# A retention layer and a feed-forward in one kernel: the order of work in the two-chunk group and two places in the load queue

## The chip, the cores and the metric

The kernel runs on one core of one Trainium2 chip. The metric is the device time of one execution in microseconds. A core has five engines with an instruction queue each: TensorE (PE; its weight loads are shown as PEld), VectorE (DVE), ScalarE (ACT), GpSimd (POOL) and SyncE (SP). Transfers are issued by POOL or SP and carried out by 16 DMA engines. Each queue runs in its program order, so an instruction that waits holds up all that stand behind it.

## What is computed

```python
B, H, S, D = 4, 8, 768, 64
gamma = 1.0 - 2.0 ** (-5.0 - np.arange(H))
for t in range(S):                                   # linear attention with decay
    state = gamma * state + np.einsum('bhd,bhe->bhde', k[:, :, t], v[:, :, t])
    y[:, :, t] = 1/sqrt(D) * np.einsum('bhd,bhde->bhe', q[:, :, t], state)
x = y.transpose(0, 2, 1, 3).reshape(B * S, H * D)    # 3072 x 512
h = x @ w_in                                         # 512 x 2048
g = h + sin(alpha * h) ** 2 / (alpha + 1e-9)
out = g @ w_out                                      # 2048 x 512
```

All inputs are float32 in memory and are cast to bfloat16 as they are loaded.

## The kernel before

The recurrence is cut into 24 chunks of 128 time steps, six for each of the four batches. `order`, also called `P`, is the order in which chunks are worked on: first the first chunk of every batch (`e0` to `e3`), then the other five of batch 0, of batch 1 and so on. P[n] is the n-th chunk in this order, counted from 0. The feed-forward takes the chunks in groups of 4, 2, 4, 4, 4, 4 and 2; the second group, the two-chunk group, is P[4] and P[5]. While the feed-forward of one group runs, the attention of the next group's chunks is worked in between; during the two-chunk group these are P[6] to P[9].

A chunk passes through these steps:

- `load_chunk` issues three DMAs on POOL's queue, for q, k and v. The last nine wide chunks (`load_seq`) come with eight DMAs for each of q, k and v of a batch. POOL keeps at most eight loads in flight: each issue waits until the eighth last has landed.
- `scale_v` multiplies v by a decay table in place, mostly on POOL, in the same queue as the loads. It waits until v has landed.
- q and k are turned (transposed), either by `turn`, a DMA transpose on SP's queue that waits until k has landed (written `X` in the schedule), or by `stage_T`, eight transposes on PE into the PSUM bank "ty" and a copy by DVE (L251; written `T`).
- `stage_A` (`A`) makes the scores, eight matmuls (L265) into the PSUM tile `pa` of two banks, which DVE multiplies by a mask (L269). For wide chunks `scores` does it (L337).
- `stage_M` (`M`) is the mix: eight matmuls with the state (L299) and eight with the scores (L303) into a tile `py` in the bank "ty", then the update of the state (L279). DVE multiplies `py` by a decay table into `xT`, the input of the feed-forward (L310), and ACT copies the state (L286). `SK` is the update of the state alone, for a chunk whose mix is done earlier.

The feed-forward of a group goes in slots. A slot (class `Slot`) is one or two slices of 128 of the 2048 inner columns: matmuls with `w_in` into a bank `ph` of the tag "mm" (L425), the sine on ACT (L428) and, by `sq`, the square on ACT (L433); `add` is the addition of h on DVE into `gT` (L440, once for each slice). The two-chunk group has eight slots of two slices. `phase` runs a group: for each slot the matmuls, sine and square, then the attention steps listed for this slot, then the slot's additions, then some matmuls with `w_out` (L450) for the group before. The order of the program is the order of every engine's queue; it is written out by hand, and tiles alone decide who waits.

PSUM has eight banks: four of the tag "mm", one "ty", one "ps" and the two of "pa". The "mm" banks hold the slots' `ph` and the output sums `po`; a new tile takes the bank that came free first. In the program's order the next group's first `ph` takes the bank of slot 5, the first output sum of the two-chunk group that of slot 6, and the next group's second `ph` that of slot 7.

The scores of a chunk of the next groups, P[10], P[11], P[12] and P[13], are made in slots 1, 5, 8 and 11 of the third group, those of P[14] in its slot 14, and those of P[15], the first wide chunk, in slot 2 of the fourth.

Of the kernel before, what the change touches and what calls it, by code (L numbers as in the profile page):

```python
# [8 lines left out]
F32 = mybir.dt.float32  # L9
# [6 lines left out]
def kernel(  # L16
# [15 lines left out]
    nc = tc.nc  # L32
# [4 lines left out]
    NP = H // 2  # L37
# [20 lines left out]
    psum = ctx.enter_context(tc.tile_pool(name="psum", bufs=1, space=bass.MemoryType.PSUM))  # L58
# [10 lines left out]
    def chunk_of(t, j):  # L69
        b, c = divmod(j, NCH)  # L70
        return t[b, :, c * C:(c + 1) * C, :].rearrange("h s d -> s h d")

    def load_chunk(j, names="qkv"):
        for name, src in (("q", q), ("k", k), ("v", v)):
            if name not in names:
                continue
            if name == "v":
                t = big.tile([128, H, D], BF16, name="vr", tag="vr", bufs=NJ - 9)
            else:
                if ("qk", j) not in raw:  # L80
                    raw["qk", j] = big.tile([128, 2, H, D], BF16, name="qkr", tag="qkr", bufs=NJ - 10)
                t = raw["qk", j][:, "qk".index(name)]
            nc.gpsimd.dma_start(out=t, in_=chunk_of(src, j))  # L83
            raw[name, j] = t

    def wide(j):
        return j >= 2 * NCH + 2 and j != 3 * NCH
# [45 lines left out]
    def scale_v(j, eng):  # L133
        t, by = raw["v", j], kg
        if wide(j):
            t, by = t.rearrange("i f p d -> i (f p) d"), kgq
        eng.tensor_mul(t, t, by[:, j % NCH, :, None].to_broadcast([128, H, D]))  # L137
# [103 lines left out]
    def stage_T(j, eng=None, tag="ty"):  # L241
        pt = psum.tile([128, 2 * NP, 128], BF16, name="pt", tag=tag, bufs=4 if tag == "mm" else 1)
        st["qkT", j] = work.tile([128, 2 * NP, 128], BF16, name="qkT", tag="qkT", bufs=6)
        for i in range(2):
            for p in range(NP):
                nc.tensor.transpose(pt[:, i * NP + p, :],
                                    raw["qk"[i], j][:, 2 * p:2 * p + 2, :].rearrange("p h d -> p (h d)"), ident)
        if eng is nc.scalar:
            nc.scalar.copy(st["qkT", j], pt)
        else:  # L250
            nc.vector.tensor_copy(st["qkT", j], pt)  # L251

    def turn(j):

        st["qkT", j] = work.tile([128, 2 * NP, 128], BF16, name="qkT", tag="qkT", bufs=6)
        nc.sync.dma_start_transpose(out=st["qkT", j], in_=raw["qk", j].rearrange(
            "i a f p d -> i (a f p d)" if wide(j) else "i a h d -> i (a h d)"))

    def stage_A(j):
        qkT = st["qkT", j]  # L260
        pa = psum.tile([128, 2, NP, 128], F32, name="pa", tag="pa")
        for p in range(NP):
            for e in range(2):
                r = slice(64 * e, 64 * e + 64)
                nc.tensor.matmul(pa[:, e, p, :], qkT[r, NP + p, :], qkT[r, p, :],  # L265
                                 start=(p == 0), stop=True, skip_group_check=True)
        aT = work.tile([128, 2, NP, 128], BF16, name="aT", tag="aT", bufs=2)
        m = dec.rearrange("p e n t -> p (e n) t") if j % NCH == 0 else mask_bc
        nc.vector.tensor_mul(aT.rearrange("p e n t -> p (e n) t"), pa.rearrange("p e n t -> p (e n) t"), m)  # L269
        st["aT", j] = aT  # L270

    def stage_S(j):
        c = j % NCH
        if c == 0:
            st["ps"] = psum.tile([128, NP, D], F32, name="ps", tag="ps")
        ps = st["ps"]
        for p in range(NP):
            for e in range(2):
                nc.tensor.matmul(ps[64 * e:64 * e + 64, p, :], raw["k", j][:, 2 * p + e, :], raw["v", j][:, 2 * p + e, :],  # L279
                                 start=(c == 0 and p == 0), stop=True, skip_group_check=True)  # L280
        return ps

    def keep_S(j, ps):
        for e in range(2):
            r = slice(64 * e, 64 * e + 64)
            nc.scalar.copy(s_bd[(j % NCH + 1) % 2][r, :, r], ps[r, :, :])  # L286

    def stage_M(j):
        c = j % NCH
        g, i = place[j]  # L290
        if g not in xT:
            xT[g] = work.tile([128, KS, sizes[g] * C], BF16, name="xT", tag="xT", bufs=3)
        qkT, aT, vs = st["qkT", j], st["aT", j], raw["v", j]
        py = psum.tile([128, NP, 128], F32, name="py", tag="ty")
        if c > 0:
            for p in range(NP):
                for e in range(2):
                    r = slice(64 * e, 64 * e + 64)
                    nc.tensor.matmul(py[r, p, :], s_bd[c % 2][:, p, r], qkT[:, p, :],  # L299
                                     start=(p == 0), stop=True, skip_group_check=True)  # L300
        for p in range(NP):
            for e in range(2):
                nc.tensor.matmul(py[64 * e:64 * e + 64, p, :], vs[:, 2 * p + e, :], aT[:, e, p, :],  # L303
                                 start=(c == 0 and p == 0), stop=True, skip_group_check=True)
        x = xT[g][:, :, i * C:(i + 1) * C]
        if c == 0:
            nc.scalar.copy(x, py)  # L307
            return
        ps = stage_S(j) if c < NCH - 1 else None
        nc.vector.tensor_mul(x, py, qg[:, c])  # L310
        if ps is not None:
            keep_S(j, ps)
# [90 lines left out]
    def run(more, *kinds):  # L403
        for kind in kinds:
            if more and kind in more:
                more.pop(kind)()
# [76 lines left out]
    def out_pieces(g, tss):  # L483
        return [lambda ts=ts, f=f: ff_out(g, ts, f) for ts in tss for f in range(FF)]
# [13 lines left out]
    e0, e1, e2, e3 = order[:B]  # L498
# [17 lines left out]
    half_T(e1, 1, nc.vector)  # L516
    nc.tensor.transpose(pal, alpha_row, ident_f)
    stage_M(e0)
    grow(1)
    idle_work(1)  # L520
# [4 lines left out]
    idle_work(2)  # L525
    half_T(e2, 1, nc.vector)
    stage_M(e1)
    grow(3)
    nc.scalar.copy(alpha_sb, pal)
# [4 lines left out]
    decay_table(1)  # L534
    idle_work(5)
    stage_M(e2)
    decay_table(2)
    idle_work(3)
# [1 line left out]

    rest = [{}]

    def phase(g, outs, att, nf=1):


        no, done = len(outs), 0
        for n in range(FF // nf):
            more, fresh = rest[0], {}
            now = Slot(g, n * nf, nf=nf).sq("A")
            run(more, "keep", "exit", "hand")  # L550
            for fn in att.get(n, ()):
                fresh.update(fn() or {})
            run(fresh, "mask")
            if fresh:
                rest[0] = fresh
            now.add()
            while done < no * (n + 1) * nf // FF:
                outs[done]()
                done += 1

    def T(j):
        return lambda: stage_T(j)

    def X(j):
        return lambda: turn(j)

    def A(j):
        return lambda: stage_A(j)

    def M(j):  # L570
        return lambda: stage_M(j)

    def SK(j):
        return lambda: keep_S(j, stage_S(j))
# [3 lines left out]
    P = order  # L578
# [9 lines left out]
    outs = out_pieces(0, (2, 3))  # L588
# [83 lines left out]
    scale_v(P[6], nc.gpsimd)  # L672
    load_chunk(P[9])
    scale_v(P[7], nc.gpsimd)
    load_chunk(P[10])
    scale_v(P[8], nc.gpsimd)
    scale_v(e1, nc.gpsimd)
    for n in range(11, 15):
        scale_v(P[n - 2], nc.gpsimd)
        load_chunk(P[n])  # L680
    load_seq(2, "q")
# [21 lines left out]
    stage_M(P[5])  # L703
    fill(4)
    phase(1, outs,
          {0: [X(P[8])], 1: [A(P[6])], 2: [T(P[7]), X(P[9])], 3: [A(P[7]), M(P[6])], 4: [X(P[10])],
           5: [A(P[8]), M(P[7])], 6: [X(P[11]), A(P[9]), M(P[8]), SK(e1)], 7: [M(P[9])]}, 2)

    where = {10: (2, 1)}
    for g in range(2, NG - 1):  # L710
# [35 lines left out]
    for g in range(2, NG):  # L746
        phase(g, out_pieces(g - 1, range(sizes[g - 1])), atts[g], 1 if sizes[g] > 2 else 2)
# [31 lines left out]
```

## Time and profile before

| | |
|---|---|
| time, median of 3 runs | 215.21 us (214.86 to 215.47) |
| span of the profiled execution, first to last instruction | 214.1 us |
| median time less this span (the profiled execution's own time is not listed apart) | 1.1 us |
| PE busy in the span | 204.8 us, 96% |
| two-chunk group, slots | 48.3 to 65.0 us |
| third group | 65.0 to about 96 us |
| granted clock of PE | 1.00 in all these stretches |
| share of the 16 DMA engines, 48.28 to 65.00 and 65.00 to 95.36 us | 1.89 and 1.95 (packets overlap on an engine, so that it exceeds 1) |

In the rows of the timeline the first two figures are the start and the length in microseconds, then come engine, line of the program, operation, what it writes and reads, and the shapes. What stands in brackets is the engine's idle time ahead of it and who ended that. A trailing x8 means that eight instructions in a row are merged. A row of the table by stretches has the stretch, its length, then the busy time of PE, PEld, DVE, ACT and POOL with the number of instructions, the granted clock, the share of the DMA engines and GB/s.

### The profile page before, as it was taken

The numbers are of one execution on the slowest core, as the hardware profiler recorded it, in microseconds if no ns is written. First come the engines' busy times: TensorE is split into PE (matmuls) and PEld (weight loads), VectorE is DVE, ScalarE is ACT, GpSimd is POOL, SyncE is SP. The second block draws the span as 40 slices with busy tenths as digits, with TensorE's granted clock in tenths as the row PEclk, the third lists the DMA queues.
The fourth block names the chain that finished last, engine by engine and source line by source line (L and its number), as shares of the span: only waits on it lengthen the run. The fifth ranks groups of instructions, "written<-read, shape, count | busy, mean of one in ns | idle before, by whom it ended". The sixth has DMA issues, their size and how long they took to land.

```text
span 214.1 us, 4691 instructions
## 1 busy us (share of the span) xinstructions
PE 204.8 (96%) x1849; PEld 109.2 (51%) x1849; DVE 131.8 (62%) x249; ACT 160.2 (75%) x303; POOL 103.5 (48%) x136
## 2 busy tenths in 40 slices
PE   7698899999999999999999999999999999999994
PEld 3344554457664555544554554554545444655653
DVE  4877859964896777746745756665744644433310
ACT  7588696758889988897697796677678787666631
POOL 8965434899679869999997103203300100000000
PEclk9999999999999999999999999999999999999999
DMA  9999999999999999999999842131011101111112
GB/s 127 147 193 186 206 207 171 154 135 229 163 148 201 126 142 187 94 147 198 170 162 145 123 98 70 32 98 54 0 51 52 40 9 52 49 49 52 49 49 98
DMA packets 101189, 24.95 MB, mean 117 GB/s; under 512 B 93728, under 2 KB 98224, under 8 KB 101168
## 3 DMA queue, kind: packets, MB, share of 16 engines
q0 software_dynamic: 77360, 13.38, 83.6%
q1 hardware_dynamic: 23664, 11.22, 25.7%
q8 instruction: 14, 0.23, 0.4%
q10 hardware_dynamic: 144, 0.07, 0.1%
q14 instruction: 7, 0.06, 0.1%
HBM read 27.27 MB, written 6.29 MB: 157 GB/s over the span
## 4 chain that ended last, share of the span: by engine, by line
PE 79%; DVE 9%; ACT 7%; DMA 3%; issue 2%; DVEq 0%; ACTq 0%
PE po L450 34%; PE ph L425 31%; ACT s L428 4%; DVE aT L269 3%; PE spare L492 3%; DMA qkT<-qk_seq 3%; DVE gT L440 2%; ACT s L433 2%; PE pa L265 2%; PE poh L473 2%; PE py L299 1%; PE py L303 1%; PE pa L337 1%; PE py L327 1%; DVE xT L310 1%
## 5 line engine op out<-in xcount | busy, mean ns | idle before, releaser
L440 DVE SCALAR_TENSOR_TENSOR gT<-s,rec_alpha,ph 128x512 bf16<-128x512 f32 (+3 forms) x120 | 74.2, 638 | 64.9 <-ACT s L433 64.8
L425 PE MATMUL ph<-xT,w_in 128*128 128x512 bf16 (+3 forms) x480 | 98.0, 336 | 0.4 <-DVE gT L440 0.2
L450 PE MATMUL po<-w_out,gT 128*128 128x512 bf16 x368 | 95.3, 380 | 0.4 <-ACT xT L307 0.3
L428 ACT ACTIVATE s<-ph,alpha_sb 128x512 f32<-128x512 f32 (+3 forms) x120 | 69.6, 601 | 34.0 <-PE ph L425 33.7
L425 PEld LDWEIGHTS <-w_in 128*128 128x128 bf16 x480 | 45.6, 98 | 41.9 <-issue 1.4
L433 ACT ACTIVATE s<-s 128x512 f32<-128x512 f32 (+1 forms) x94 | 58.4, 621 | 2.6
L450 PEld LDWEIGHTS <-gT 128*128 128x128 bf16 x368 | 33.9, 98 | 36.4 <-issue 0.6
L391 POOL CAST s_bd<-s_f 64x256 bf16<-64x256 f32 x10 | 3.9, 394 | 39.5 <-DVE s_f L384 30.1
L462 ACT COPY o_sb<-po 128x512 f32<-128x512 f32 x23 | 13.2, 579 | 4.0 <-PE po L450 3.9
L83 POOL DMA_DIRECT2D vr<-in_v_dram x15 | 13.7, 914 | 3.4 <-DMA w_in<-in_moe_w_in_dram 1.7
L83 POOL DMA_DIRECT2D qkr<-in_q_dram x14 | 12.8, 917 | 3.8 <-DMA w_out<-in_moe_w_out_dram 1.6
L137 POOL TENSOR_TENSOR vr<-vr,kg 128x512 bf16<-128x512 bf16 x12 | 12.7, 1071 | 3.8 <-DMA vr<-in_v_dram 3.3
L83 POOL DMA_DIRECT2D qkr<-in_k_dram x14 | 12.5, 896 | 3.7 <-DMA w_out<-in_moe_w_out_dram 3.3
L269 DVE TENSOR_TENSOR aT<-pa,mask 128x1024 bf16<-128x1024 f32 x11 | 13.4, 1218 | 0.5 <-PE pa L265 0.5
L103 POOL DMA_DIRECT2D qk_seq<-in_q_dram x16 | 11.3, 741 | 2.9 <-DMA qkr<-in_k_dram 1.2
L137 POOL TENSOR_TENSOR v_seq<-v_seq,kgq 128x512 bf16<-128x512 bf16 x9 | 9.4, 1071 | 4.0 <-DMA v_seq<-in_v_dram 3.7
L103 POOL DMA_DIRECT2D v_seq<-in_v_dram x16 | 11.3, 776 | 0.0
L103 POOL DMA_DIRECT2D qk_seq<-in_k_dram x16 | 11.2, 743 | 0.0
L492 PE MATMUL spare<-warm 128*128 128x512 bf16 x28 | 9.5, 462 | 1.2 <-DVE warm L156 1.2
L286 ACT CAST s_bd<-ps 64x256 bf16<-64x256 f32 x24 | 8.7, 361 | 2.3 <-PE ps L279 2.1
L346 DVE TENSOR_TENSOR aTw<-pa,maskq 128x768 bf16<-128x768 f32 x9 | 8.6, 955 | 0.7
L310 DVE TENSOR_TENSOR xT<-py,qg 128x512 bf16<-128x512 f32 x11 | 7.5, 685 | 1.8 <-PE py L303 1.7
(92 smaller groups left out, 143.0 us busy)
## 6 DMA issues: line engine op xcount, KB each, us to landing
out_dram<-o_sb SPq DMA_DIRECT2D x23, 256.0 KB, 2.2
w_in<-in_moe_w_in_dram POOLq DMA_DIRECT2D x4, 512.0 KB, 11.3
w_out<-in_moe_w_out_dram POOLq DMA_DIRECT2D x4, 512.0 KB, 14.9
vr<-in_v_dram POOLq DMA_DIRECT2D x15, 128.0 KB, 7.0
qkr<-in_q_dram POOLq DMA_DIRECT2D x14, 128.0 KB, 7.0
qkr<-in_k_dram POOLq DMA_DIRECT2D x14, 128.0 KB, 7.4
qk_seq<-in_q_dram POOLq DMA_DIRECT2D x8, 80.0 KB, 6.7
qk_seq<-in_k_dram POOLq DMA_DIRECT2D x8, 80.0 KB, 4.6
```

The lines of the kernel that those rows point to most:

```text
L83: nc.gpsimd.dma_start(out=t, in_=chunk_of(src, j))
L103: nc.gpsimd.dma_start(out=o, in_=src[bt, h, cs[0] * C:, :].rearrange("(f i) d -> i f d", i=64))
L137: eng.tensor_mul(t, t, by[:, j % NCH, :, None].to_broadcast([128, H, D]))
L269: nc.vector.tensor_mul(aT.rearrange("p e n t -> p (e n) t"), pa.rearrange("p e n t -> p (e n) t"), m)
L310: nc.vector.tensor_mul(x, py, qg[:, c])
L425: nc.tensor.matmul(self.ph[:, m, :], w_in[:, i, f * 128:(f + 1) * 128], xT[g][:, i, self.lo:self.hi], start=(m == 0 and i == 0), stop=(i = ...
L428: nc.scalar.activation(out=self.s[:, m, :], in_=self.ph[:, m, :], func=ACTF.Sin, scale=alpha_sb[:, f:f + 1])
L433: nc.scalar.activation(out=self.s, in_=self.s, func=ACTF.Square)
L440: nc.vector.scalar_tensor_tensor(gT[self.g][:, f, self.lo:self.hi], self.s[:, m, :], rec_alpha[:, f:f + 1], self.ph[:, m, :], op0=ALU.mult ...
L450: nc.tensor.matmul(po[g, ts], gT[g][:, f, ts * C:(ts + 1) * C], w_out[:, f, :], start=(f == 0), stop=(f == FF - 1))
L462: nc.scalar.copy(o_sb, po[g, ts])
L492: nc.tensor.matmul(spare["ps"], warm[:, :128], warm, start=True, stop=True)
```

## The change

It does four things, all in or ahead of the two-chunk group.

- The mix of P[9], the last one in the group (slot 7), takes its PSUM tile from the tag "pa", the scores' two banks, and no longer from "ty".
- The additions of slot 6 are held back: `phase` keeps them and issues them in slot 7 after that slot's attention steps, so behind the multiplication that ends the mix of P[9], and ahead of slot 7's own additions.
- P[7] (the chunk `T` stands for; the eighth chunk counted from one) is turned by PE in slot 0 instead of slot 2.
- In POOL's queue the three loads of P[10] are put behind the scalings of v of P[8], of `e1` and of P[9]. Those of P[11] still follow them, now behind P[10]'s; the scaling of P[10] comes after both.

```diff
-    def stage_M(j):
+    def stage_M(j, tag="ty"):
...
-        py = psum.tile([128, NP, 128], F32, name="py", tag="ty")
+        py = psum.tile([128, NP, 128], F32, name="py", tag=tag)
...
-    def phase(g, outs, att, nf=1):
+    def phase(g, outs, att, nf=1, late=None):
...
+        held = None
...
-            now.add()
+            if held is not None:
+                held.add()
+                held = None
+            if n == late:
+                held = now
+            else:
+                now.add()
...
     scale_v(P[7], nc.gpsimd)
-    load_chunk(P[10])
     scale_v(P[8], nc.gpsimd)
     scale_v(e1, nc.gpsimd)
-    for n in range(11, 15):
+    scale_v(P[9], nc.gpsimd)
+    load_chunk(P[10])
+    load_chunk(P[11])
+    for n in range(12, 15):
         scale_v(P[n - 2], nc.gpsimd)
         load_chunk(P[n])
...
     phase(1, outs,
-          {0: [X(P[8])], 1: [A(P[6])], 2: [T(P[7]), X(P[9])], 3: [A(P[7]), M(P[6])], 4: [X(P[10])],
-           5: [A(P[8]), M(P[7])], 6: [X(P[11]), A(P[9]), M(P[8]), SK(e1)], 7: [M(P[9])]}, 2)
+          {0: [X(P[8]), T(P[7])], 1: [A(P[6])], 2: [X(P[9])], 3: [A(P[7]), M(P[6])], 4: [X(P[10])],
+           5: [A(P[8]), M(P[7])], 6: [X(P[11]), A(P[9]), M(P[8]), SK(e1)],
+           7: [lambda: stage_M(P[9], "pa")]}, 2, 6)
```

## The prediction, made before the changed kernel ran

> **What bounds the kernel now.** I read the engines' busy shares first, then the busy table by stretches, then the timeline of the two-chunk group (48.3 to 65.0 us) and of the stretch behind it.
>
> ```profile
> PE 204.8 (96%) x1849; PEld 109.2 (51%) x1849; DVE 131.8 (62%) x249; ACT 160.2 (75%) x303; POOL 103.5 (48%) x136
> 48.28:65.00 16.72, 15.99 (x217) 11.53 (x216) 13.27 (x24) 14.26 (x33) 13.43 (x15) 1.00 1.89 180
> 65.00:95.36 30.36, 30.15 (x254) 14.59 (x253) 21.55 (x29) 27.56 (x50) 27.59 (x38) 1.00 1.95 148
> 95.36:182.00 86.64, 86.64 (x827) 42.81 (x828) 50.70 (x89) 65.98 (x109) 29.70 (x43) 1.00 0.66 85
> ```
>
> The second figure of the last three rows is the stretch's length, the third PE's busy time. PE loses 0.73 us in the group, 0.21 us in the next stretch and nothing from 95.36 to 182 us, at a granted clock of 1.00. So the change, which touches neither the matmuls nor the end, can at best win about 0.9 us. The timeline shows where that idle time lies and who ends it:
>
> ```profile
> 54.34 0.40 PE L265 MATMUL pa<-qkT 64*128 64x128 bf16 x8 [0.22 <-DVE qkT L251]
> 62.85 0.68 DVE L310 TENSOR_TENSOR xT<-py,qg 128x512 bf16<-128x512 f32 x1
> 63.45 0.86 DVE L440 SCALAR_TENSOR_TENSOR gT<-s,rec_alpha,ph 128x256 bf16<-128x256 f32 x2
> 63.58 0.41 PE L299 MATMUL py<-qkT,s_bd 128*64 128x128 bf16 x8 [0.34 <-DVE xT L310]
> 64.26 0.69 DVE L310 TENSOR_TENSOR xT<-py,qg 128x512 bf16<-128x512 f32 x1
> 64.86 0.86 DVE L440 SCALAR_TENSOR_TENSOR gT<-s,rec_alpha,ph 128x256 bf16<-128x256 f32 x2
> 65.00 1.02 PE L425 MATMUL ph<-xT,w_in 128*128 128x512 bf16 x4
> 95.36 0.25 PE L337 MATMUL pa<-qkT 64*64 64x128 bf16 x4 [0.21 <-DMA qkT<-qk_seq]
> ```
>
> There are four gaps: 0.22 us ahead of the scores of P[7], which wait for DVE's copy of its turned q and k; 0.34 us ahead of the mix of P[9], which waits until DVE has read the mix of P[8] out of the one "ty" bank; 0.12 us (64.88 to 65.00) ahead of the next group's first projection, which waits for x of P[9]; 0.21 us at 95.36, where the scores of P[15] wait for a transpose by DMA. That transpose hangs on the loads, so POOL's queue and SP's come next:
>
> ```profile
> 55.23 1.04 POOL L137 TENSOR_TENSOR vr<-vr,kg 128x512 bf16<-128x512 bf16 x1 [1.71 <-DMA vr<-in_v_dram]
> 59.61 1.04 POOL L137 TENSOR_TENSOR vr<-vr,kg 128x512 bf16<-128x512 bf16 x1 [0.69 <-DMA vr<-in_v_dram]
> 64.19 1.04 POOL L137 TENSOR_TENSOR vr<-vr,kg 128x512 bf16<-128x512 bf16 x1 [0.88 <-DMA vr<-in_v_dram]
> 74.55 0.68 POOL L103 DMA_DIRECT2D qk_seq<-in_q_dram  x1 [0.91 <-DMA qkr<-in_k_dram]
> 81.77 5.48 POOL L103 DMA_DIRECT2D qk_seq<-in_k_dram  x8
> 89.87 2.94 SPq L256 DMA_TRANSPOSE qkT<-qk_seq  x2
> ```
>
> POOL scales, issues, waits for landings and issues again; the last of the wide k loads goes out at 86.49 us and takes 3.2 us, SP turns P[15] at 89.87, and that takes 5.4 us: 95.3.
>
> **Part by part.** The sum is made on this execution's span of 214.1 us; the median of the runs, 215.21 us, lies 1.1 us above it, and I carry the difference over unchanged.
>
> *Turning P[7] in slot 0.* The eight transposes (0.61 us on PE) and DVE's copy (0.69 us) move two slots ahead. PE's work is only reordered; its place in slot 0 is free, since "ty" was last read at 48.1. DVE's copy falls at about 50.0, inside 2.8 us in which DVE waits for ACT (to 50.89). In slot 3 the scores follow the projection at once: minus 0.22 us. The scores of P[8] then come at 57.94 instead of 58.16, and their transpose lands at 58.1 now (issued 49.59, 8.5 us). This gain would be lost but for the moved loads: the three loads of P[10] (issued 48.76 to 51.46) no longer lie on the engines beside it. Loads that follow each other land 0.9 us apart, so up to 2.7 us of engine time goes from in front of the transposes of P[8] and P[9].
>
> *Mix of P[9] in the scores' bank.* Its PE work is the same. It needs the mask of P[9] finished (62.93, less 0.22: 62.71) and the state's copies (62.85, less 0.22: 62.63); PE has ended the projection of slot 7 at 63.24, less 0.22: 63.02. So it starts there, 0.56 us ahead of now. An undisturbed mix is followed by DVE's multiplication 0.68 us later (95.65 to 96.33): 63.70, instead of 64.26.
>
> *Additions held back.* This multiplication now runs ahead of slot 6's additions: 63.70 to 64.39, and the next group's projection follows at 64.43 instead of 65.00: 0.57 us, the 0.22 included. But queued behind it on DVE stand both pairs of additions. A pair takes 0.81 us to the next instruction's start and the multiplication 0.60, so slot 6's run from 64.30 and slot 7's from 65.11 to 65.97. Now they end at 65.72, since DVE does not stand idle from 63.31 to 63.70 as it will. Who waits: the four "mm" banks go round in the order in which they come free, so the second projection of the next group takes slot 7's bank. It could start at 65.72 (66.29 less 0.57) and has to wait until about 66.01. That returns 0.29 us; what is left of the group's gain is 0.28 us.
>
> *Two chunks' loads.* POOL's issues of P[10] move past the scalings of P[8], of the second batch's first chunk and of P[9], whose wait for the landing at 55.2 stays. P[10] goes out from 56.2 instead of 48.8, P[11] from 58.9 instead of 56.2, ending at 61.6. The scaling of P[10] comes at 61.7 instead of 59.61, P[12] goes out 2.1 us later than now, and with the waits of 0.69 and 0.88 us gone P[14] about 1.4 us later (its issues end at 73.0 instead of 71.6). SP waits for k of P[10] at its transpose, and behind that stands only the one of P[11], which waits for its own k anyway.
>
> Two things hang on this. First, the transpose of P[10], needed at 66.97 (67.25 less 0.28). Its k goes out at 57.15, where P[11]'s goes now; a wide load on quiet engines takes 2.7 us and P[11]'s k took 6.4, so it lands between 59.9 and 63.6. I take 61.0, as P[10] then follows two transposes alone. A transpose takes 5.2 to 8.5 us in this stage, 5.4 outside a queue of loads; I take 5.2, the row (63.64) that like this one has less than a chunk in front: 66.4, in time by half a microsecond. The other end is 72.1, 4.9 us later than now needed.
>
> Here the order of landing counts: the transpose issued at 53.89 landed at 60.6, behind all loads that POOL had issued before it (the last at 50.56, landed 59.5). The Trainium skill, DMA: Bandwidth & Descriptors, section "Queues, rings and completion order", says that an engine takes packets from its queues in turns; by that alone the transpose of P[10] would share with P[11]'s loads from its first packet on and land about 1 us sooner (an estimate from that page's rule), which would leave the sum as it is and make the rival "P[10] late" below less likely. The trace agrees only in part, as the landings in order of issue show.
>
> Second, the wide loads. They wait at 74.55 to 79.09 for earlier landings, 2.7 us in five waits. The 1.4 us fit into these if the loads of P[13] and P[14] land when they do now. The engines have the same bytes to move and were never idle (DMA share 1.89 and 1.95 in the two stretches), so I take these landings as unchanged: the transpose of P[15] lands at 95.3, as now. Its bounds: 1.4 us later, if landings follow POOL's shift; 1.3 us earlier, if the waits disappear (2.7 less 1.4).
>
> **Sum.** PE reaches 95.36 with 0.28 us won and waits 0.49 us there instead of 0.21. Nothing is won at the end: 215.2 us. The cap, with a transpose landing early enough, is minus 0.49 us.
>
> **Rivals.**
> *All stalls go* (0.17). The transpose of P[15] lands earlier and the wait for slot 7's additions is smaller than I reckon: up to minus 0.89 us, 214.3. For it: the five waits of POOL leave room for 1.3 us. Against it: the order of DVE's queue.
> *The wide loads come later* (0.22). If P[14] lands 1.4 us later, each step down to the transpose of P[15] moves, PE waits until 96.75 instead of 95.36, and nothing after it gives time back: 216.6. It decides from 0.65 us of delay on. For it: POOL issues 1.4 us later, and P[14]'s loads took 7.8 us to land. Against it: this much is queue, and a shorter queue takes it up.
> *P[10] late* (0.13): its transpose lands after it is needed. With the median 7.0 us and a k at 61.9 it lands at 69.0, and PE stands at the scores of P[10] until then instead of 67.25: plus 1.8 us, 217.0. It decides from a landing at 67.9 on.
>
> **How the numbers follow.** About 0.3%, 0.65 us, is what a measurement here can tell from no change. The forecast, within it, has 0.48; its own range is 214.7 (minus 0.49) to 215.8. Faster 0.17 is the first rival, slower 0.35 the other two. The range runs from 214.5, short of the first rival's full gain, to 216.6.
>
> **What would show it.** Right: no gap ahead of the scores of P[7]; mix of P[9] at about 63.0 and the projection behind it at 64.4; a new gap of 0.3 us ahead of the second projection; the gap at the scores of P[15] twice as long. Wrong: a gap ahead of the scores of P[8], P[9], P[10] or P[13] that a transpose ends; wide k loads whose first issue is more than half a microsecond from 81.77; PE busy from 65 to 95 without a gap and 0.5 us ahead.

## The result, and the profile after

The changed kernel is slower: 218.94 us, median of 6 runs (217.74 to 222.82), against 215.34 (214.86 to 216.16) for the kernel before, run beside it; the ratio is 1.0149, 95% interval 1.0117 to 1.0181, so about 3.2 us. Forecast were 215.2 us, with a range of 214.5 to 216.6. The ratios here leave out runs more than 1.5% above the fastest of their kernel, whatever made them long, so a ratio can differ from that of the medians.

A run's time lies 1.8 us above its span (the profiled one of the changed kernel: 217.92 and 216.1), not the 1.1 that I took from the median. The execution shown of before was thus one of about 215.9 us, and that of the changed kernel is the second fastest of six: between the two traces stand 2.0 us, not 3.2. Counted from the first projection of the two-chunk group to the last instruction it is 2.5 us (165.8 and 168.3), since the changed one entered the group earlier.

The first lines of the profile and the table by stretches of the changed kernel, with the columns of before:

```profile
PE 204.6 (95%) x1849; PEld 108.4 (50%) x1849; DVE 132.0 (61%) x249; ACT 160.2 (74%) x303; POOL 103.5 (48%) x136
48.28:65.00 16.72, 16.44 (x219) 11.56 (x218) 13.95 (x25) 14.67 (x34) 9.88 (x12) 1.00 1.52 152
65.00:95.36 30.36, 29.14 (x248) 13.99 (x245) 21.02 (x28) 26.44 (x48) 28.11 (x37) 1.00 1.67 150
95.36:182.00 86.64, 84.56 (x801) 41.70 (x802) 49.72 (x88) 64.91 (x107) 32.55 (x46) 1.00 0.72 89
```

PE does the same work. It idles less in the group (0.28 us instead of 0.73: 0.16 ahead of the mix of P[8], which waits for DVE to read that of P[7], and 0.12 ahead of the next group's projection) and more behind it: 1.22 and 2.08 us, where before had 0.21 and nothing. The share of the DMA engines in the first two rows fell from 1.89 and 1.95 to 1.52 and 1.67. The timeline of the changed kernel:

```profile
60.25 0.41 PE L299 MATMUL py<-qkT,s_bd 128*64 128x128 bf16 x8 [0.16 <-DVE xT L310]
62.35 0.41 PE L299 MATMUL py<-qkT,s_bd 128*64 128x128 bf16 x8
63.03 0.69 DVE L310 TENSOR_TENSOR xT<-py,qg 128x512 bf16<-128x512 f32 x1 [0.32 <-PE py L303]
63.64 1.64 DVE L440 SCALAR_TENSOR_TENSOR gT<-s,rec_alpha,ph 128x256 bf16<-128x256 f32 x4
63.77 1.02 PE L425 MATMUL ph<-xT,w_in 128*128 128x512 bf16 x4
65.26 1.02 PE L425 MATMUL ph<-xT,w_in 128*128 128x512 bf16 x4
67.43 0.40 PE L265 MATMUL pa<-qkT 64*128 64x128 bf16 x8 [1.15 <-DMA qkT<-qkr]
97.44 0.25 PE L337 MATMUL pa<-qkT 64*64 64x128 bf16 x4 [2.12 <-DMA qkT<-qk_seq]
```

This execution enters the group 0.52 us earlier than that of before (first projection at 47.76 instead of 48.28), which is to be added to times of PE and DVE when the two are set side by side. POOL's queue is only 0.13 us earlier (the scaling at 47.64 instead of 47.77), so its times are compared as they stand. The edits of the slots do what they say: the mix of P[9] starts without a wait, its multiplication runs ahead of the four held additions, and the second projection is at 65.78 on the scale of before, 0.51 us earlier. Then two transposes by DMA end long gaps: that of P[10] (1.15 us) and that of P[15] (2.12 us). POOL's queue says why they come late:

```profile
47.64 1.08 POOL L137 TENSOR_TENSOR vr<-vr,kg 128x512 bf16<-128x512 bf16 x1
49.02 2.05 POOL L137 TENSOR_TENSOR vr<-vr,kg 128x512 bf16<-128x512 bf16 x2 [0.31 <-DMA vr<-in_v_dram]
56.53 1.04 POOL L137 TENSOR_TENSOR vr<-vr,kg 128x512 bf16<-128x512 bf16 x1 [5.46 <-DMA vr<-in_v_dram]
57.52 0.94 POOL L83 DMA_DIRECT2D qkr<-in_q_dram  x1
63.91 1.04 POOL L137 TENSOR_TENSOR vr<-vr,kg 128x512 bf16<-128x512 bf16 x1 [1.07 <-DMA vr<-in_v_dram]
73.44 1.04 POOL L137 TENSOR_TENSOR vr<-vr,kg 128x512 bf16<-128x512 bf16 x1 [2.16 <-DMA vr<-in_v_dram]
84.68 5.49 POOL L103 DMA_DIRECT2D qk_seq<-in_k_dram  x8
```

POOL stands 5.46 us in front of the scaling of P[9], and the loads of P[10] stand behind it: they go out at 57.52, 8.8 us later than before. The first wide k load goes out at 84.68 instead of 81.77. Between 57 and 59 us the DMA engines have almost nothing to do. The table for this stretch, before and after (the last two figures are the engines' share and GB/s):

```profile
57.00:59.00 2.00, 1.98 (x38) 1.42 (x37) 1.16 (x4) 1.97 (x5) 1.92 (x3) 1.00 2.47 148
```

```profile
57.00:59.00 2.00, 2.00 (x40) 1.39 (x39) 1.65 (x4) 1.97 (x5) 2.00 (x3) 1.00 0.13 30
```

From 54 to 62 us the engines moved 1262 KB before and 705 KB after (rates by lengths of the stretches 54 to 57, 57 to 59 and 59 to 62). The missing 557 KB are 3.7 us of their work at 150 GB/s. By 96 us some 380 KB are still missing (159 and 151 GB/s from 48 to 96 us).

An empty stretch alone does not tell the two kernels apart, though: the kernel before has two microseconds of the same kind further on.

```profile
63.00:64.00 1.00, 0.66 (x18) 0.52 (x17) 1.00 (x3) 0.72 (x2) 0.30 (x1) 1.00 0.27 41
72.00:73.00 1.00, 1.00 (x11) 0.34 (x11) 0.52 (x1) 0.97 (x3) 1.00 (x3) 1.00 0.34 11
```

What differs is POOL's own time. From its scaling at 47.64 us (47.77 before) to the first wide k load it takes 37.0 us instead of 34.0, since it waits 9.0 us in all on the way and not 6.0.

### The profile page after: what moved, and what is told of

Its sections match the earlier page's. It is cut to its first block, busy times and chain, and to the rows that moved or that the text cites. A ratio compares the mean times of both kernels' runs of the same rounds, so it can differ in the third digit from the quotient of the medians.

```text
span 216.1 us, 4691 instructions
## 1 busy us (share of the span) xinstructions
PE 204.6 (95%) x1849; PEld 108.4 (50%) x1849; DVE 132.0 (61%) x249; ACT 160.2 (74%) x303; POOL 103.5 (48%) x136
## 4 chain that ended last, share of the span: by engine, by line
PE 76%; DMA 8%; ACT 6%; DVE 4%; POOL 3%; issue 1%; POOLq 0%; DVEq 0%; ACTq 0%
PE po L450 34%; PE ph L425 33%; DMA w_in<-in_moe_w_in_dram 3%; ACT s L428 3%; DMA qkT<-qk_seq 2%; DMA qkT<-qkr 2%; ACT s L433 2%; PE pa L265 2%; PE poh L473 2%; POOL qkr L83 2%; PE py L299 1%; DVE aT L269 1%; POOL vr L83 1%; PE pa L337 1%; PE py L327 1%
## 5 line engine op out<-in xcount | busy, mean ns | idle before, releaser
L492 PE MATMUL spare<-warm 128*128 128x512 bf16 x28 | 8.9, 436 | 1.2 <-DVE warm L156 1.2
```

The source lines that it names most:

```text
L492: nc.tensor.matmul(spare["ps"], warm[:, :128], warm, start=True, stop=True)
```

## The experiments

The theory after the result, called the dry-queue theory: the loads of P[10] go out so late that the DMA engines run out of work, and every transfer behind them, the transposes of P[10] and P[15] included, comes late. The rivals: the edits of the slots cost the time; the displacement as such costs, in proportion; or POOL's wait for a landing does.

**Only the loads moved.**

```diff
     scale_v(P[7], nc.gpsimd)
-    load_chunk(P[10])
     scale_v(P[8], nc.gpsimd)
     scale_v(e1, nc.gpsimd)
-    for n in range(11, 15):
+    scale_v(P[9], nc.gpsimd)
+    load_chunk(P[10])
+    load_chunk(P[11])
+    for n in range(12, 15):
```

> Only the two chunks' loads are moved; the group's slots are as before. Dry-queue theory (POOL waits for v of P[9] with no load issued behind it, the DMA engines run out of work, every later load and with it the transposes of P[10] and P[15] come late): the whole loss, a ratio of 1.013 to 1.018, POOL's idle time ahead of the scaling of P[9] about 5 us instead of 1.7, first wide k load about 3 us later than before, PE gap ahead of the scores of P[15] over 2 us. Rival, the slots' edits cost it (held additions, the mix in the scores' bank): within 0.4% of before.

Measured: 1.0155 (1.0119 to 1.0191), the whole loss. The profiled execution was the fastest of its six (217.36 us), and its figures are smaller than expected: 3.09 us of waiting ahead of the scaling, first wide k load at 84.05, a gap of 0.96 us at the scores of P[15]. The loads of P[10] went out at 54.99, and the nearly empty stretch is one microsecond (19 GB/s from 56 to 57 us; 117 GB/s from 57 to 59). From the group's start to the end this execution takes 1.5 us more than that of before; where the longer runs lose the rest is not shown.

```profile
54.01 1.04 POOL L137 TENSOR_TENSOR vr<-vr,kg 128x512 bf16<-128x512 bf16 x1 [3.09 <-DMA vr<-in_v_dram]
```

**Only the slots edited.** Turn of P[7] in slot 0, mix in "pa", additions held, loads as before.

> The three edits of the slots (turn in slot 0, mix in the scores' bank, additions held back) without the moved loads. Dry-queue theory: no loss; PE reaches the third group 0.5 us early, loses part of it ahead of the second projection, and the gap at the scores of P[15] grows by what is left; ratio 0.997 to 1.001. Rival, the slots' edits cost it: 1.005 or more, with PE gaps inside the group that the kernel before does not have.

Measured: 1.0025 (1.0001 to 1.0049): no gain, perhaps a small loss, just above what I expected. The three gaps in and behind the group are gone, but two others have come, which transposes by DMA end, 0.45 us ahead of the scores of P[8] and 1.10 us ahead of those of P[9]:

```profile
58.40 0.40 PE L265 MATMUL pa<-qkT 64*128 64x128 bf16 x8 [0.45 <-DMA qkT<-qkr]
62.00 0.40 PE L265 MATMUL pa<-qkT 64*128 64x128 bf16 x8 [1.10 <-DMA qkT<-qkr]
```

PE is earlier, the transposes are not, so the gain is waited away in the group itself and not only at P[15]. Gaps inside the group were a sign that I had given to the rival, but their price is far below the 1.005 that it asked for. Part of the 1.10 us belongs to this execution: POOL had issued the loads of P[9] 1.3 us later than in the first trace (46.36 instead of 45.08).

**Past two scalings, not past the one that waits.**

```diff
     scale_v(P[8], nc.gpsimd)
     scale_v(e1, nc.gpsimd)
-    scale_v(P[9], nc.gpsimd)
     load_chunk(P[10])
-    load_chunk(P[11])
-    for n in range(12, 15):
+    for n in range(11, 15):
         scale_v(P[n - 2], nc.gpsimd)
         load_chunk(P[n])
```

> As the changed kernel, but the loads of P[10] go out after the scalings of P[8] and of the second batch's first chunk and ahead of that of P[9], so they pass two scalings (2 us of POOL) and no wait for a landing. Dry-queue theory: what costs is the wait, so nearly all comes back: ratio 0.998 to 1.004, POOL's idle ahead of the scaling of P[9] 1 us or less. Rival, what counts is how far the loads are put back (2 us of the 7 to 8 us): a ratio of 1.004 to 1.008.

Measured: 1.0009 (0.9984 to 1.0034). The loss is gone, and a cost in proportion to the displacement lies outside the interval. POOL's wait ahead of the scaling of P[9] was still 3.00 us, more than I had said, but the loads were out already (from 52.05), and the engines were busy: 138 GB/s from 57 to 59 us. The gap ahead of the scores of P[9] is there too (1.05 us).

**Slots without held additions**, loads as before (the slots' edits less `late`):

> Turn in slot 0 and mix in the scores' bank alone: no held additions, loads as before. By the order of VectorE's queue the first projection of the third group comes 0.3 us later than with held additions (about 64.75 on the scale of before), but the second one has no wait for slot 7's additions and the scores of P[10] come 0.4 us earlier than with them. End: the transpose of P[15] decides as in the kernel with held additions, so the same time within 0.15%; ratio 0.996 to 1.000. If held additions help as such, this kernel is slower than that one by 0.1% or more.

Measured: 1.0011 (0.9988 to 1.0033), not told apart from the kernel with held additions; here too the transposes of P[8] and P[9] end gaps (0.28 and 0.82 us).

**v of P[9] loaded first**, in the changed kernel, so that POOL's wait is shorter:

```diff
-    load_chunk(P[9])
+    load_chunk(P[9], "vqk")        # load_chunk issues in the order of the names
```

> The changed kernel with the order of POOL's queue kept (the loads of P[10] still behind all three scalings), but the load of P[9] issues v first and then q and k, so that v lands about 2.5 us earlier in the row of loads. That takes the wait away and leaves the displacement. Dry-queue theory: POOL's idle time ahead of the scaling of P[9] falls from 5.5 us to 2 or 3 us, the stretch of nearly idle DMA engines around 58 us goes, and two thirds of the loss or more comes back: ratio 0.999 to 1.006. Rival, the number of scalings passed counts, or the order of P[10] behind the transposes: 1.010 or more, as in the changed kernel.

Measured: 1.0160 (1.0102 to 1.0219), from the two shortest of six runs; the median of all six is 221.07 us, against 215.58 beside it. The wait fell to 2.14 us as expected, the loss did not: an expectation missed. The trace shows another mechanism. k of P[9], now last, landed at 55.95, so SP issued the transpose of P[9] at 56.09, behind the q and k loads of P[10] (54.44 and 55.37). It landed 8.1 us later, and PE stood 3.90 us in front of the scores of P[9]. The stretch from 57 to 59 us is filled again (122 GB/s), as expected, but since another loss took its place, the run says nothing for or against the theory of the empty queue. It shows one transpose that was issued behind two loads and landed late.

**P[9] too turned by PE**, in slot 4, loads as before, without and with held additions:

```diff
-          2: [X(P[9])], ... 4: [X(P[10])],
+          4: [T(P[9]), X(P[10])],
```

> Turn of P[7] in slot 0 and mix in the scores' bank, loads as before, and P[9] too turned on TensorE (in slot 4, copy by VectorE) instead of by DMA. In the three kernels with the early slots and early loads the scores of P[9] had a gap of 0.8 to 1.1 us ahead of them that the DMA transpose of P[9] ended, so the transposes bind as soon as TensorE is earlier. Theory: the gap goes, the DMA engines have 256 KB less to move and everything behind lands 1 to 2 us earlier, at 0.45 us more TensorE work: ratio 0.994 to 0.999. Rival, the gain is bound elsewhere (the transposes of P[13] or P[15]) or VectorE's extra 0.7 us delays the group: 1.000 to 1.004.

> The same with slot 6's additions held back. With the transposes out of the way VectorE's order alone decides: by it the first projection of the third group comes 0.3 us earlier and the second has to wait for slot 7's additions, so that the scores of P[10] come 0.4 us later than without: 0.1 to 0.2% slower than the kernel without held additions. Rival, held additions help (the earlier first projection is kept): 0.1 to 0.2% faster.

Measured: 1.0019 (0.9994 to 1.0044) and 1.0034 (1.0010 to 1.0057). Both lie above what I had expected of the first (0.994 to 0.999), in the range of its rival. The gap at P[9] is gone in both; what was won went into 0.45 us of transposes on PE and a wait of 0.49 us of these for the "ty" bank. Whether holding additions helps or hurts the two do not tell: the intervals overlap.

**The loads of P[10] put back by POOL's own work.** Two multiplications of a scratch tile, then six, on top of the kernel that passes two scalings:

```diff
     scale_v(P[8], nc.gpsimd)
     scale_v(e1, nc.gpsimd)
+    pad = consts.tile([128, H, D], BF16, name="pad")
+    nc.gpsimd.memset(pad, 0.0)
+    for _ in range(2):             # 6 in the other
+        nc.gpsimd.tensor_mul(pad, pad, kg[:, 0, :, None].to_broadcast([128, H, D]))
     load_chunk(P[10])
     for n in range(11, 15):
```

> The three edits of the slots, and the loads of P[10] put back by POOL's own work instead of by a wait: they go out after the scalings of P[8] and of the second batch's first chunk and two multiplications of a scratch tile (together some 4.4 us), ahead of the scaling of P[9]. Theory, put as a threshold: before, a k load issued in this place landed after 9.1 us, on quiet engines it lands after 3.7 to 4.5 us, so there are about 4.8 us of queue in front, and a load put back by less than that loses nothing; besides the DMA transpose of P[9] now goes ahead of P[10], so the gap of 1 us ahead of the scores of P[9] goes: ratio 0.997 to 1.002. Rival, every microsecond of displacement costs in proportion (3.3 us lost for some 8 us): 1.006 to 1.009.

> The same with six multiplications of the scratch tile: the loads of P[10] go out some 8.6 us late, as in the changed kernel, but POOL never waits there for a landing: it works, and the scaling of P[9] stands behind these loads. Theory (the DMA engines run out of work, whatever keeps POOL from issuing): the loss of the changed kernel or somewhat more, ratio 1.013 to 1.025, and the same stretch of nearly idle DMA engines around 57 to 59 us. Rival, it is the wait for the landing of v of P[9] that costs as such: ratio under 1.006.

Measured: 0.9996 (0.9961 to 1.0031) with two, 1.0236 (1.0182 to 1.0291) with six. So the loss needs no wait for a landing. With six, POOL works without a break, the loads go out at 58.19, and the engines are as empty as in the changed kernel; the scores of P[10] wait 3.41 us:

```profile
57.00:59.00 2.00, 2.00 (x41) 1.38 (x39) 1.65 (x4) 1.94 (x6) 1.92 (x3) 1.00 0.03 8
69.83 0.40 PE L265 MATMUL pa<-qkT 64*128 64x128 bf16 x8 [3.41 <-DMA qkT<-qkr]
```

With two they go out at 53.79, 5 us later than in the first trace, and the engines stay busy:

```profile
57.00:59.00 2.00, 2.00 (x41) 1.38 (x39) 1.65 (x4) 1.94 (x6) 2.00 (x3) 1.00 2.11 133
```

POOL's time fits both. Before, its waits up to the first wide k load were 6.0 us. The two multiplications and the clearing of the tile, 2.7 us, come mostly out of these waits: 3.9 us of them are left, and that load goes out 34.6 us after the scaling of P[7] (34.0 before). Six, with the clearing 7.2 us, are more than the waits can give: 2.2 us are left, and the load goes out after 37.3 us, about as late as in the changed kernel (37.0).

The profiled execution with two has no gap over 0.2 us behind the group's start and takes 165.1 us from there to the end, 0.7 less than before; the cap of my prediction was 0.89. But its runs lie far apart, 214.62 to 221.66, where those of the kernel before beside it went from 214.86 to 217.86. Without held additions:

> The kernel with the loads 4.4 us late, without the held additions. If the transposes are out of the way in it, VectorE's order alone tells the two apart, and this one is faster by 0.1 to 0.2%; ratio 0.995 to 1.001. If the transposes still bind, both take the same time.

Measured: 1.0017 (0.9973 to 1.0061), not faster than with held additions; the median of all twelve runs is 217.91 us, against 215.53 beside it. The profiled execution is one of its long ones (220.34 us), and shows where such a run loses its time:

```profile
63.52 0.61 PE L265 MATMUL pa<-qkT 64*128 64x128 bf16 x8 [4.24 <-DMA qkT<-qkr]
```

Here k of P[9] landed at 55.38, after the loads of P[10] had begun to go out (53.74); the transpose was issued at 55.52 and landed 8.0 us later. In the short execution with held additions it was issued at 53.69, a tenth of a microsecond ahead of the loads, and landed after 4.8 us. The two executions differ in more than that order: k of P[9] itself landed 9.4 us after its issue in the long one and 7.9 us in the short one.

**Loads of P[10] tied to the landing of k of P[9]**, so that this order is certain, again on top of the kernel that passes two scalings:

```diff
     scale_v(e1, nc.gpsimd)
+    mark = consts.tile([128, D], BF16, name="mark")
+    nc.gpsimd.tensor_copy(mark, raw["k", P[9]][:, 0, :])
     load_chunk(P[10])
```

> The three edits of the slots; the loads of P[10] go out as soon as k of P[9] has landed (a small copy out of that tile on POOL holds them until then), ahead of the scaling of P[9]. So SP's transpose of P[9], which waits for the same landing, is always issued ahead of them, and they are put back by about 5 us, near the edge at which the engines run dry. Theory (transfers are served in the order of issue, so a transpose issued behind these three loads lands 8 us after its issue and one ahead of them 4 to 5 us): no gap ahead of the scores of P[9], and the runs lie closer together than those with the loads 4.4 us late; ratio 0.995 to 1.000, the fastest of all kernels here. Rival, 5 us already drains the engines: 1.003 to 1.008 with a gap at the scores of P[10] or P[15].

> The same without held additions. With no transpose in the way VectorE's order alone is left: the first projection of the third group 0.3 us later, no wait ahead of the second, so 0.1 to 0.2% faster than with held additions; ratio 0.994 to 1.000. Rival, a transpose decides further on in both: the same time within 0.1%.

Measured: 1.0029 (0.9995 to 1.0063) and 1.0021 (0.9990 to 1.0052), both above the 1.000 that I had expected at most. No kernel here is shown to beat the one before. In the two traces the gap at P[9] is gone (its transpose landed 4.8 and 4.9 us after issue) and one of them is short, 164.9 us from the group's first projection to the end (165.8 before); the other, where the loads went out only at 55.27, has 1.08 us ahead of the scores of P[15]. But the runs lie as far apart as without the tie (214.98 to 220.10 with held additions), so the order of that one transpose is not all that spreads them. What else does stays open.

## Why the prediction was wrong, point by point

*What bounds the kernel, and the cap.* Right as far as the traces show: counted from the group's first projection, the shortest took 164.9 and 165.1 us, 0.9 and 0.7 less than the 165.8 of before, against a cap of 0.89. The spans do not show it, since the one of 214.1 us belongs to a run longer than the median of its kernel; in none of the measured kernels was the gain kept in the median.

*Turn of P[7], mix in the scores' bank, held additions.* Right in direction and nearly in size. Said were the mix at 63.02, the projection at 64.43 and the second at 66.01; measured, with 0.52 added, 62.87, 64.29 and 65.78. The new wait for slot 7's additions is there but nearer 0.2 than 0.29 us: the spacing of the two projections grew from 1.29 to 1.49 us. That the gain would be lost without moving the loads, because the transpose of P[8] only just came in time, fits the kernel with the slots' edits alone (0.45 us of waiting there); that of P[9] was the worse, with 1.10 us.

*Transposes of P[8] and P[9] freed.* Right: they land at 56.9 and 57.8 instead of 58.1 and 60.6, and no gap stands at their scores.

*The loads.* Here the prediction failed, in one sentence: "The engines have the same bytes to move and were never idle (DMA share 1.89 and 1.95 in the two stretches), so I take these landings as unchanged." The shares are averages, and they hide that the engines did run nearly empty at 63 and 72 us. Nor did the landings stay: they followed POOL's issues, and the last of the wide k loads landed at 92.3 instead of 89.7. Loads of this kind landed up to 9 us after their issue before, but in 3.4 to 4.5 on quiet engines (3.38 and 4.47 us in the kernel with six multiplications), so some 5 us of queue lay in front of the loads of P[10]. Put back by 4.4 to 5 us, these loads lose little (a ratio of 0.9996, though the runs spread); by 8.8 they leave the engines empty from 57 to 59 us. I had the displacement on paper, 48.8 to 56.2, and did not set it against the depth of the queue.

*The terms that follow from it.* POOL's last issue for P[14] was to be 1.4 us late and was 5.5 us late (77.1 instead of 71.6). The sum had mis-sized POOL's waits: the one ahead of the scaling of P[9], "whose wait for the landing at 55.2 stays", ended at 56.5; the scaling of P[10], taken to run at once, waited 1.07 us; and while the 0.88 us ahead of the scaling of P[11] did go, 2.16 us came ahead of that of P[12]. The five waits at the wide loads did take up 2.7 us of this, as I had said, and 2.9 us were left: the first wide k load was that much late, outside my bounds of minus 1.3 to plus 1.4, and the transpose of P[15] landed 2.1 us late. That of P[10] was taken to land in time by half a microsecond, and came 1.15 us late. Its k went out at 58.45 instead of 57.15 and took 4.5 us, where I had reckoned with 3.9, between P[11]'s 6.4 and the 2.7 of a wide load half as large; so it landed at 62.9 instead of 61.0. The transpose itself took 4.3 us, less than the 5.2 of the sum. So P[10] came late by the late issue of its loads and not by a queue in front of them.

*Rivals.* "The wide loads come later" named the mechanism, but capped it at 1.4 us, and "P[10] late" came with it and not instead of it. Both were one cause, and their prices should have been on one line.

*The page on packets taken in turns.* The Trainium skill, DMA: Bandwidth & Descriptors, "Queues, rings and completion order", would let a transpose share from its first packet on. The traces do not fit this for a block of loads issued ahead: the transpose of P[9] landed 8.0 and 8.1 us after its issue behind two loads of P[10], and 4.8 to 4.9 us in the three traces in which it was issued just ahead of them. No run isolates that order, since other landings shifted with it.

## What to carry to other kernels

Before moving a load back, set the distance against the depth of the queue in front of it: the time from issue to landing now, less the same on quiet engines. Here 5 us of queue stood in front; a move of up to 5 us cost little in the ratio, and one of about 9 us cost 1.5 to 2.4%. Count the time of the issuing engine as well: its waits are what a delay can be taken from, and what exceeds them arrives at every later transfer. And do not take landings as unchanged when the loads ahead of them move.

## What the runs showed of the hardware that I had not expected

A long gap costs PE more than itself. In the kernel with six multiplications PE stood 3.41 us in front of the scores of P[10], and the table by stretches shows the granted clock (the figure ahead of the last two) after it:

```profile
66.00:70.30 4.30, 0.89 (x11) 0.34 (x10) 0.78 (x2) 1.81 (x3) 2.68 (x4) 1.00 2.23 157
70.30:73.70 3.40, 3.40 (x9) 1.18 (x8) 1.85 (x2) 0.83 (x2) 3.40 (x5) 0.50 1.48 200
73.70:76.00 2.30, 2.30 (x12) 1.02 (x11) 0.75 (x1) 1.81 (x4) 2.30 (x3) 1.00 1.56 136
```

Half the clock for 3.4 us is 1.7 us more. The same came with the gaps of 3.90 us (v of P[9] loaded first) and 4.24 us (there for some 6.8 us); none came with the gaps of 1.15 and 2.12 us. The Trainium skill, TensorE: Matmul & The Clock Gate, "Part 1: The HAM clock gate", states half rate after an idle window of about 3.4 us. These traces agree. All six runs of the kernel with six multiplications have a mean granted clock of 0.982 to 0.992. Two of the six runs of the changed kernel, of 220.2 and 222.8 us, had a mean granted clock of 0.991 and 0.992 instead of 0.998 to 1.000, which fits one such stretch each; they were not profiled, so this part of the difference between the trace's 2.0 us (2.5 from the group's start) and the measured 3.2 is inferred, not shown.
